# Attention and a top-k expert layer on one core: values in shorter pieces, wider DVE transposes, guard sums on two engines, and a new written order

## The chip, the cores and the metric

The kernel runs on one core of a Trainium2 chip. The metric is device time in microseconds (us): the median of several runs, and beside it one execution that the hardware profiler recorded. TensorE is called PE here (its weight loads PEld), VectorE DVE, ScalarE ACT, GpSimd POOL, SyncE SP.

## The reference

Attention over 8 batches of 8 heads, 576 tokens and 64 dimensions in float32, with rotary positions; then, in every batch, the 128 tokens with the highest gate score go through a two-layer network and are added back.

```python
q_rot, k_rot = rotate(q), rotate(k)
scores = scale * np.matmul(q_rot, k_rot.transpose(0, 1, 3, 2))
scores = scores - np.max(scores, axis=-1, keepdims=True)
attn = np.exp(scores)
attn = attn / (np.sum(attn, axis=-1, keepdims=True) + 1e-09)
x = np.matmul(attn, v)                       # per head, then heads side by side: (8, 576, 512)
...
scores[b] = x[b] @ w_gate
top_idx = np.argpartition(-scores[b], capacity)[:capacity]       # capacity = 128
h = np.maximum(x[b, top_idx] @ w1, 0.0)      # 512 -> 1024
out[b, top_idx] = x[b, top_idx] + sigmoid(scores[b, top_idx])[:, None] * (h @ w2)
```

## The kernel before

**Groups and units.** The 64 heads are worked in 16 groups of four (two groups make a batch), and a group is two pairs of heads, c = 0 and 1. A group has nine *units* u of 64 query columns for each pair. For a unit, `units` issues the score matmuls of both pairs (16 instructions on PE in tiles of 64x64, names `k_in` and `q_in`). For each of the two pairs `softmax` then drains the scores from PSUM, takes the row minimum of the negated scores (`nm`) and lets ACT make the exponentials with their sums (`prob`, `sums`). The table `DRAINS` says how a pair's unit is drained: "V" is one DVE instruction that drains and takes the minimum at once; "S" is a drain on ACT and a DVE reduction after it.

**Transposes.** The exponentials are transposed in place by DVE in 32x32 blocks, one instruction for both pairs of a unit (128x1152 elements); in the first units of groups 0 and 1 (`APART`) one for each pair.

**Values.** When all units of a group are transposed, `value` multiplies with the values: 18 key blocks, accumulated in four banks of PSUM, in tiles of 32x64 (names `prob`, `vt`), given to the order as three operations of six key blocks (96 matmul instructions each). ACT or DVE copies the sum out (`ot`), PE transposes it back with an identity (names `ident,ot`, whole array), and ACT or DVE scales the rows into `x`, by the reciprocals of the sums plus 1e-9: the *guard sums* (`guarded`, four small ACT additions, name `rs`) and a DVE reciprocal.

**Experts.** Behind every second group `route` and `chosen` pick the tokens (PE: `sc`, `past`, `tok`), POOL gathers their rows, and PE runs the two layers (names `xt,w1t` and `w2t,ht`, whole array). POOL also rotates k and q (`rotate`: a product with the table `tabk`, then an addition), and multiplies rows with the gate.

**What sets the order.** Nothing is scheduled at run time. All steps are recorded as operations, and the table `LINES` gives for each engine the order in which its operations stand, written as numbers in base 64. Every engine's queue is in order, and waits on semaphores for what the others make. `Order.run` replays that order with assumed durations; what it decides is which of the eight PSUM banks an operation gets. Its constants (`FETCH`, `SWITCH`, a restart price) are no part of the program that runs.

Almost all instructions carry the line of the helper that records them (L238 before, L243 after), so the rows below are told apart by tiles and shapes.

Of the kernel before, what the change touches and what calls it, by code (L numbers as in the profile page):

```python
# [13 lines left out]
ALU = mybir.AluOpType  # L14
# [11 lines left out]
BLOCK, FETCH = 256, 3600.0  # L26
# [13 lines left out]
6Z7B7t767364637I688O8R8W8Z95926c944L8Y978-6h8Q9c8T6j9e9b9i9k7H7G6l9n4K9x9p9A9E9r9v9C7U9K9I7W4PaJaG7YaB9RawaOaRau4Sb0aAb2  # L40
aIaLaTaDaQb8baaZbgbdaX9Q9PblbicFcCbpcScXcHbfbnb4cUcNd28rcRcEbw9WcZc-d6a1cLd9d4dca3dedjdbdidlbvbudwbBeh8qdreqdpdvdyelep8v
ejeBewbKeydFeDeFeseLeRePdDdEeUeJgodKgneYeWf1dR8ygtdTgqf3f0dVgvf7f9gxfggBgJcfgGgDgLgWgOgRg+gIgTh3gYh2h5gQhah9hcfeffhhhgi2
hjflici9i4ieibikiiiphqi6irfwioixivhphoiHiJhtiBiDkehCk7iNk9hEcmkliPhGkdkgiVknksiTkrkzkuf-kyj0kkkFkHkMkBkLkOkUkSi-i+kZkYk-
j5f+malNm1lYm9jcm5m3l6mclLlTmhlRl+mglXmnl4l5mjmtmpjglbmvg3mAldmCnSmznQlinYg6o2odmJo8o6lknWo0lmjLojocoqofopolovosoxozoDoF
mImHprpojKmMoMpxpqmZptpFpDoKoLpIpRpKoRpzpQpZpWpMjPq4pToPq6q3p-oYrzpYrxqcqarFqfo+qhqjrKqqrRnsp0rJrMrDrQrTrWr+rYs2s4qoqps7
sbs9qxnrsfskqCsnt2qEsht1t4nwtmqGt8tdsmtotattspnztBtytltItftvtAtDswtHthtstQtKtTtVtOsvtXsuu2szsBsIu0u1r9r8rduyrguxuC""",
    "DVE": """
0r0s0v0w0t0u0x0z0y0A0C0R0I0+0T1f17100K1o1h191q1x1A1H1F1b1C131j1O1J0W150N1l1M1t0Y331d2V1Q3a0P1v2G38351X3i2+2L2Q2I3f3p2X3n
3c3k2S3u3x3r303E3z3C5C3M3J595F3O5f5d573G5w5y5J5L2N5j5s5q5S5h5m5Z5Q5N5H5b5A5X5U5o6T6R3V6J6M6+5u6V797b5-7o7m726O7i7s7u667g
6Y7y7A4v7q757k4C4y4B4A4z7w704E7d6a7C8P774H8X937J968S8+4M989a909d8U9h9j9f9l9u9w9q7P9o9D7L7N9H9B9Jat9Fav9L9saH8baz9S9yaC8h  # L50
8g8f8i8eb3aSb1aWaYaKaxb9aPb7aMaEaUbha+bbbobm9U8kcGcQcDbecKcMcYcTc+8nbjb5d3bqd59YcI4Xd0cVcOd7dddabxdhdka5dfdmdodudqbz8sek
eibDdxeoevexbIdsdzeEemeCerezeIeKbMeGeteQb-eOdGeSeXeVgmc2dIc5c6gpdMc3eMe-c4eZf2gwf6f8c8gugrf4gAgygCcbfhfagKcg8DgZgEgPgHgS
gXgMh1h4g-h6h8hbgUhdhfhii5fjcefnhki3idiaihijfsiffuiqinili7hriwiuisiyiIfLiGhxiAiCiKhviOiMcjiEkck6k8kffOfSfPfRfQkjkmfUiUka
khiSkqktiWiQkxfXkEkGkvj1kAcrkIkKkNkokCkTkRg0kPkVkXk+lKlMj7j3l0m8m4lWlQm2lSmblZm6mfmdjemilOmmmolUl7l-msmumkmqnRl9nPmwmyjv
mBnXnVjyjzjAn-o1jBjCmDobnTo7o5jEjFo9oeoiokmKjHnZgbooo3orogjMoyowomotoAoCoEoGmOmQmVpwmXpyoNpspppEncpCpupGpLpJpPninfoTngnj
pSnhpAp+pNpXq5q2pUnlryrwq7qbjSq0q9rErAqdnoqiqgrCrIqkjXrPrSqrrLrNrGrZrUrXs1s3r-s5sas8sesgqvqtsct0slsot3t9t7sit5nttktgqVte
# [59 lines left out]
class Order:  # L116
# [36 lines left out]
    def run(self):  # L153
# [19 lines left out]
        while events:  # L173
# [4 lines left out]
            while moved:  # L178
                moved = False
                for e, line in lines.items():  # L180
                    while free[e] <= t and place[e] < len(line) and not line[place[e]].waits and able(e, line[place[e]]) <= t:
# [8 lines left out]
                        if e == "PE":  # L190
                            begin += SWITCH[mode][o.mode] + 70.0 * (t > free[e] + 1)
# [27 lines left out]
                        for n in o.outs:  # L219
                            n.ready = max(n.ready, o.end + self.SEM)  # L220
# [91 lines left out]
def attention_moe_kernel(ctx: ExitStack, tc: tile.TileContext, q, k, v, w_gate, w1, w2, rope, outs, cap):  # L312
# [67 lines left out]
    def pe(ns):  # L380
        return {"PE": (ns, ns + 165)}
# [77 lines left out]
    for t_ in rss.tiles:  # L459
# [5 lines left out]
    APART = {0: 6, 1: 3}  # L465
    DRAINS = (
        ("VVVVVSVSS", "SSSVVSSVV"),
        ("VSSSSSSSS", "SSSVSVSVS"),
        ("SVVVVVVSS", "VVSVVSVVV"),
        ("VSSVVSVVV", "SVVSVVVVV"),  # L470
        ("SSSVVSVSV", "SSSSVVVVV"),
        ("VVSSVSVSS", "VSSSVVVSV"),
        ("SVVSSSVVV", "SVSVVSSVS"),
        ("SVVSVVSVV", "VSVVVVVSV"),
        ("VSVSSSVVV", "SVVSSVSSS"),
        ("SSVVVVVVV", "VSVSVVVVV"),
        ("VVVVVVVVV", "VSSSSVSVS"),
        ("VVVSVVVVV", "VVSVSSVVS"),
        ("VVVVVVVSV", "VVVVSVSVV"),
        ("SVVSVSVVS", "SVVVSSSVV"),  # L480
        ("VVVVSVSVS", "VVSSVVVVS"),
        ("VVSVVSVVS", "SVVSSSSVV"),
# [38 lines left out]
    def rotate(pi):  # L521
# [12 lines left out]
        for name, use, tab, cuts in (("k", kin, tabk, CUTS), ("q", qin, tabk, QCUTS)):  # L534
            x = use.tile
# [519 lines left out]
```

## Time and profile before

| what | before |
|---|---|
| median of 3 runs | 514.68 us (513.63 to 515.67) |
| the profiled execution: its own time, its span | 514.91 us, 513.2 us |
| PE busy | 484.9 us, 94% |
| DVE busy | 449.5 us, 88% |
| ACT busy | 389.8 us, 76% |
| POOL busy | 340.8 us, 66% |
| granted PE clock, mean | 0.993 |

The profiled execution's own time is 1.7 us longer than the span from its first to its last instruction. Busy shares are means over the whole span; the windows further down give them by stage.

### The profile page before, as it was taken

How to read it: one execution, taken by the hardware profiler on the slowest of the kernel's cores; microseconds unless marked ns; L12 is line 12 of the kernel's file. 1: busy time of each engine (PE TensorE's matmuls, PEld its weight loads, DVE VectorE, ACT ScalarE, POOL GpSimd, SP SyncE). 2: the span in 40 equal slices, each digit the busy share in tenths (PEclk: the TensorE clock that was granted, in tenths of full speed). 3: DMA queues.
4: the chain of work that ended last, by engine and by line, in shares of the span. 5: the costliest groups of instructions: out<-in, count | busy, mean ns of one | idle time of the engine just before them, and what ended most of it. 6: DMA issues, size and time to landing. Idle time of an engine off the chain costs nothing.

```text
span 513.2 us, 19024 instructions
## 1 busy us (share of the span) xinstructions
PE 484.9 (94%) x7988; PEld 301.1 (59%) x7988; DVE 449.5 (88%) x871; ACT 389.8 (76%) x1087; POOL 340.8 (66%) x268
## 2 busy tenths in 40 slices
PE   8879787989999999998999999999999999999995
PEld 7446354555675556654558455674557456656872
DVE  6999999999999999999999999999779989991701
ACT  1799999999978989697887769887658778884110
POOL 2998398798793978758686795938587596006110
PEclk9989999899999999999999999999999999999999
DMA  8867676566445556363554536245563253130310
GB/s 288 286 185 221 186 232 204 157 195 190 139 121 150 152 167 196 89 209 105 167 160 142 170 101 216 67 127 164 176 190 118 75 178 84 58 101 23 114 42 20
DMA packets 47381, 76.52 MB, mean 149 GB/s; under 512 B 4928, under 2 KB 28224, under 8 KB 47296
## 3 DMA queue, kind: packets, MB, share of 16 engines
q1 hardware_dynamic: 45472, 70.54, 45.0%
q0 software_dynamic: 1280, 4.20, 2.4%
q8 instruction: 62, 1.02, 0.8%
q10 hardware_dynamic: 544, 0.59, 0.4%
q14 instruction: 23, 0.19, 0.1%
HBM read 63.77 MB, written 11.53 MB: 147 GB/s over the span
## 4 chain that ended last, share of the span: by engine, by line
PE 64%; ACT 12%; POOL 8%; issue 7%; DVE 6%; DMA 2%; SPq 1%; POOLq 0%; DVEq 0%
PE banks L238 64%; ACT prob L238 7%; DVE prob L238 5%; POOL k_in L238 4%; POOL q_in L238 3%; ACT ot L238 2%; ACT x L238 2%; DMA k_in<-k_dram 2%; SPq L238 1%; POOL prod L238 1%; ACT rs L238 0%; DVE nm L238 0%; ACT prod L238 0%; POOLq L1050 0%; POOL xe L238 0%
## 5 line engine op out<-in xcount | busy, mean ns | idle before, releaser
L238 ACT ACTIVATE prob<-prob,nm 128x576 f32<-128x576 f32 x288 | 220.7, 771 | 39.9 <-DVE prob L238 29.4
L238 DVE STREAM_TRANSPOSE prob<-prob 128x1152 f32<-128x1152 f32 (+1 forms) x153 | 194.1, 1288 | 4.4 <-ACT prob L238 4.0
L238 PE MATMUL banks<-k_in,q_in 64*64 64x288 f32 x2304 | 180.9, 419 | 17.3 <-DVE prob L238 7.0
L238 PE MATMUL banks<-prob,vt 32*64 32x288 f32 x4608 | 151.0, 405 | 2.1 <-ACT prob L238 2.0
L238 PEld LDWEIGHTS banks<-k_in,q_in 64*64 64x64 f32 x2304 | 83.5, 134 | 101.3 <-issue 25.4
L238 DVE TENSOR_SCALAR_CACHE_REDUCE prob<-banks 128x576 f32<-128x576 f32 x174 | 125.8, 742 | 11.9 <-PE banks L238 11.2
L238 PEld LDWEIGHTS banks<-prob,vt 32*64 32x64 f32 x4608 | 98.6, 132 | 51.1 <-issue 11.7
L238 POOL TENSOR_TENSOR q_in<-q_in,tabk 128x1152 f32<-128x1152 f32 (+1 forms) x32 | 82.8, 2592 | 15.3 <-DMA q_in<-q_dram 15.2
L238 POOL TENSOR_TENSOR k_in<-k_in,tabk 128x1152 f32<-128x1152 f32 (+1 forms) x31 | 81.1, 2618 | 12.6 <-DMA k_in<-k_dram 12.1
L238 ACT ACTIVATE prob<-banks 128x576 f32<-128x576 f32 x114 | 71.5, 647 | 22.9 <-PE banks L238 22.5
L238 POOL TENSOR_TENSOR prod<-x,wg 128x512 f32<-128x512 f32 (+1 forms) x45 | 49.3, 1096 | 56.0 <-ACT prod L238 17.4
L238 DVE TENSOR_REDUCE nm<-prob 128x1 f32<-128x576 f32 x114 | 81.5, 732 | 0.2
L238 PEld LDWEIGHTS banks<-xt,w1t 128*128 128x128 f32 x512 | 59.3, 192 | 8.0 <-issue 4.9
L238 PE MATMUL banks<-xt,w1t 128*128 128x128 f32 x512 | 63.1, 278 | 0.0
L238 PE MATMUL banks<-w2t,ht 128*128 128x512 f32 x128 | 61.6, 609 | 0.3 <-ACT ht L238 0.3
L238 ACT ACTIVATION_READ_ACCUMULATOR prob<-prob,nm 128x1 f32 x288 | 55.9, 194 | 0.0
L238 POOL TENSOR_TENSOR k_in<-k_in 128x576 f32<-128x576 f32 x31 | 43.8, 1414 | 0.9
L238 POOL TENSOR_TENSOR q_in<-q_in 128x576 f32<-128x576 f32 x31 | 43.8, 1417 | 0.9
L238 POOL TENSOR_SCALAR sel<-slots,rank 128x128 bf16<-128x128 bf16 x30 | 17.6, 599 | 38.8 <-DVE rank L238 38.8
L238 ACT ACTIVATE x<-banks,rs 128x64 f32<-128x64 f32 (+1 forms) x156 | 33.5, 333 | 4.5 <-PE banks L238 2.5
L238 PEld LDWEIGHTS banks<-w2t,ht 128*128 128x128 f32 x128 | 22.0, 189 | 23.3 <-issue 21.6
L238 ACT COPY ot<-banks 128x576 f32<-128x576 f32 x32 | 18.9, 638 | 10.8 <-PE banks L238 10.5
(68 smaller groups left out, 272.4 us busy)
## 6 DMA issues: line engine op xcount, KB each, us to landing
k_in<-k_dram SPq DMA_DIRECT2D x64, 288.0 KB, 3.6
vt<-v_dram SPq DMA_DIRECT2D x96, 192.0 KB, 2.9
q_in<-q_dram SPq DMA_DIRECT2D x62, 288.0 KB, 3.6
out_dram<-x SPq DMA_DIRECT2D x32, 256.0 KB, 3.5
w1t<-w_dram SPq DMA_DIRECT2D x8, 256.0 KB, 3.5
w2t<-w_dram SPq DMA_DIRECT2D x8, 256.0 KB, 3.4
out_dram<-x SPq DMA_DIRECT2D x16, 64.0 KB, 2.2
tabk<-rope_dram ACTq DMA_DIRECT2D x2, 288.0 KB, 3.6
```

Source lines behind the costliest of these rows:

```text
L238: i = made(*args, **kwargs)
```

## The change

Four things. The values of a group are recorded as six operations of three key blocks each (`STEP = 3`) and not three of six. In groups 1 to 14 DVE transposes two units at a time (`SPAN`, new helper `turn`), 128x2304 elements. The guard sums may stand on POOL as well as on ACT; the new table puts those of 8 of the 16 groups on POOL. And `LINES` and `DRAINS` are new: "S" drains go from 114 to 146 and "V" drains from 174 to 142. In the replay, an operation of a sum that stands behind another of PE may now start as soon as PE is free.

```diff
+RESTART = (70.0, 130.0, 70.0)
...
+    SPAN = {g: 2 for g in range(1, 15)}
+    STEP = 3
...
-            part = prob.tile[:, cs[0] * NU + u:cs[-1] * NU + u + 1:NU]
-            y = op({"DVE": dve(len(cs) * S, 1, 26.0)}, lambda: nc.vector.transpose(part, part),
-                   [exps[c, u] for c in cs])
+        def turn(cs, u0, u1):
+            part = prob.tile.rearrange("p (c u) s -> p c u s", c=2)[:, cs[0]:cs[-1] + 1, u0:u1]
+            part = part[:, 0] if len(cs) == 1 else part[:, :, 0] if u1 - u0 == 1 else part
+            y = op({"DVE": dve(len(cs) * (u1 - u0) * S, 1, 26.0)}, lambda: nc.vector.transpose(part, part),
+                   [exps[c, u] for c in cs for u in range(u0, u1)])
             prob.by(y)
             turned.append(y)
...
-            for i in range(3):
-                o = op(pe(CH * 485), lambda i=i: products(i), turned + vt[i][1] + [o], acc, mode=1,
-                       words=32 * CH)
+            for k0 in range(0, NB, STEP):
+                use, got = vt[k0 // CH]
+                o = op(pe(STEP * 485), stream(k0, k0 + STEP), turned + got + [o], acc, mode=1, words=32 * STEP)
+                prob.by(o), use.by(o)
...
-                        nc.scalar.add(r[64 * half:64 * half + 64, 0:n, 2 * h:2 * h + 2].rearrange("p t c -> p c t"),
-                                      su[64 * h:64 * h + 64, :, half:NU:2], EPS)
-
-            gd = op({"ACT": (800, 905)}, guarded, list(exps.values()) + rs.before)
+                        to = r[64 * half:64 * half + 64, 0:n, 2 * h:2 * h + 2].rearrange("p t c -> p c t")
+                        of = su[64 * h:64 * h + 64, :, half:NU:2]
+                        if e == "ACT":
+                            nc.scalar.add(to, of, EPS)
+                        else:
+                            nc.gpsimd.tensor_scalar(to, of, EPS, None, op0=ALU.add)
+
+            gd = op({"ACT": (800, 905), "POOL": (560, 560)}, guarded, list(exps.values()) + rs.before)
...
         for u in range(NU):
-            for cs in ((0,), (1,)) if u < APART.get(g, 0) else ((0, 1),):
+            apart = u < APART.get(g, 0)
+            for cs in ((0,), (1,)) if apart else ((0, 1),):
                 units(cs, u)
+                if apart:
+                    turn(cs, u, u + 1)
+        lo = APART.get(g, 0)
+        while lo < NU:
+            hi = min(lo + SPAN.get(g, 1), NU)
+            turn((0, 1), lo, hi)
+            lo = hi
```

What the new order does is seen best in three places.

On PE, where the first layer of batch 4 begins (`sc` is batch 5's routing scores, `ot` the rows to be transposed back, `w1t` the first layer), there stood before one half of a token block's products, a unit of scores, and the next half:

```order
L238 MATMUL banks<-ident,sc_104 128x128 x5
L238 MATMUL banks<-ident,ot_88 128x128 x4
L238 MATMUL banks<-xt_100,w1t 128x128 x8
L238 MATMUL banks<-k_in_80,q_in_76 64x288
...
L238 MATMUL banks<-k_in_81,q_in_77 64x288
L238 MATMUL banks<-xt_100,w1t 128x128 x8
```

Now 24 of the first layer's matmuls stand together:

```order
L243 MATMUL banks<-ident,sc_104 128x128 x5
L243 MATMUL banks<-ident,ot_88 128x128 x4
L243 MATMUL banks<-ident,ot_88 64x128 x2
L243 MATMUL banks<-xt_100,w1t 128x128 x24
L243 MATMUL banks<-ident,ot_88 128x128 x4
L243 MATMUL banks<-k_in_78,q_in_74 64x288
```

The scores that stood between the pieces have gone ahead of them, into one run. Counted over all of PE's order, the changes from one tile size to another (128x128, 64x64, 32x64) go from 186 to 167: 17 fewer between scores and whole-array work, 2 fewer at values. Of the 19, 4 are gone in groups 0 to 7 and 15 in groups 8 to 15.

On DVE, in the middle of group 6 (`prob_86` is the buffer of the even groups), the transposes of two units now stand as one instruction between the drains:

```order
L243 STREAM_TRANSPOSE prob_86<-prob_86 128x2x1152
L243 TENSOR_SCALAR prob_86,nm_93<-banks 128x576 x2
L243 STREAM_TRANSPOSE prob_86<-prob_86 128x2x1152
L243 TENSOR_SCALAR prob_86,nm_93<-banks 128x576 x2
L243 STREAM_TRANSPOSE prob_86<-prob_86 128x2x1152
```

Before, no instruction of 128x2x1152 was there. Over the kernel 110 transposes of 128x2x576 become 55 of 128x2x1152; 25 of 128x2x576 and 18 of 128x576 remain.

On POOL, among the rotations of k and q for groups 1 and 2, the order before was:

```order
L238 TENSOR_TENSOR k_in_80<-k_in_80 128x576
L238 TENSOR_TENSOR k_in_78<-k_in_78,tabk 128x1152
L238 TENSOR_TENSOR k_in_78<-k_in_78 128x576
L238 TENSOR_TENSOR q_in_74<-q_in_74,tabk 128x1152
L238 TENSOR_TENSOR q_in_75<-q_in_75,tabk 128x1152
```

Now the guard sums of group 0 stand between them:

```order
L243 TENSOR_TENSOR k_in_80<-k_in_80 128x576
L243 TENSOR_TENSOR k_in_78<-k_in_78,tabk 128x1152
L243 TENSOR_SCALAR rs_95<-sums_91 64x2x5 x2
L243 TENSOR_SCALAR rs_95<-sums_91 64x2x4 x2
L243 TENSOR_TENSOR q_in_74<-q_in_74,tabk 128x1152
```

The four additions have moved from ACT's queue into POOL's, behind a rotation. Further up in POOL's queue the addition for `q_in_75` of group 0 is gone; it stands on DVE now.

## Rows read from the trace of the kernel before

**Rows 1.** Busy time by stage: window, its length, PE, PEld, DVE, ACT, POOL.

```profile
12.00:34.00 22.00, 17.06 (x150) 8.20 (x146) 22.00 (x41) 18.30 (x43) 21.84 (x13) 1.00 0.76 251
34.00:130.00 96.00, 85.39 (x1745) 50.16 (x1749) 94.13 (x166) 92.33 (x271) 77.68 (x52) 0.96 0.66 196
130.00:230.00 100.00, 98.83 (x1619) 61.94 (x1612) 95.94 (x178) 86.91 (x242) 74.20 (x60) 1.00 0.51 152
230.00:460.00 230.00, 225.40 (x3903) 138.25 (x3901) 213.87 (x409) 181.39 (x502) 151.03 (x111) 1.00 0.44 135
460.00:513.20 53.20, 47.63 (x519) 33.11 (x518) 15.86 (x56) 9.60 (x34) 13.31 (x23) 1.00 0.14 48
```

**Rows 2.** Waits, whole span: who waited for whom, us, times, longest.

```profile
DVE prob L238 <- PE banks L238: 11.2, 27, 0.9
...
PE banks L238 <- DVE prob L238: 7.0, 11, 1.8
```

**Rows 3.** Timeline of PE, value stretches: start, length, what, count.

```profile
41.14 3.17 PE L238 MATMUL banks<-prob,vt 32*64 32x288 f32 x96
44.23 1.20 PE L238 MATMUL banks<-k_in,q_in 64*64 64x288 f32 x16
...
71.73 8.99 PE L238 MATMUL banks<-prob,vt 32*64 32x288 f32 x288
80.64 1.20 PE L238 MATMUL banks<-k_in,q_in 64*64 64x288 f32 x16
```

**Rows 4.** Timeline of PE, an expert stretch.

```profile
270.71 1.95 PE L238 MATMUL banks<-xt,w1t 128*128 128x128 f32 x16
272.49 0.60 PE L238 MATMUL banks<-ident,ot 128*128 128x128 f32 x4
273.02 1.20 PE L238 MATMUL banks<-k_in,q_in 64*64 64x288 f32 x16
274.15 2.05 PE L238 MATMUL banks<-xt,w1t 128*128 128x128 f32 x16
276.14 2.17 PE L238 MATMUL banks<-k_in,q_in 64*64 64x288 f32 x32
278.24 2.05 PE L238 MATMUL banks<-xt,w1t 128*128 128x128 f32 x16
```

**Rows 5.** Timeline of DVE around 28 us.

```profile
27.48 1.36 DVE L238 STREAM_TRANSPOSE prob<-prob 128x1152 f32<-128x1152 f32 x1
...
28.77 0.70 DVE L238 TENSOR_REDUCE nm<-prob 128x1 f32<-128x576 f32 x1
...
29.41 0.76 DVE L238 STREAM_TRANSPOSE prob<-prob 128x576 f32<-128x576 f32 x1
...
30.09 0.70 DVE L238 TENSOR_REDUCE nm<-prob 128x1 f32<-128x576 f32 x1
```

**Rows 6.** Timeline of ACT around 38 us; the bracket is idle time before.

```profile
36.41 0.91 ACT L238 ACTIVATE rs<-sums 64x10 f32<-64x10 f32 x4
38.23 1.19 ACT L238 ACTIVATE prob<-banks 128x576 f32<-128x576 f32 x2 [0.90 <-PE banks L238]
```

**Rows 7.** Groups by shape, DVE and ACT: busy us, mean ns, idle before.

```profile
L238 DVE TENSOR_SCALAR_CACHE_REDUCE prob<-banks 128x576 f32<-128x576 f32 x174 | 125.8, 742 | 11.9 <-PE banks L238 11.2 <-ACT prob L238 0.2
L238 DVE TENSOR_REDUCE nm<-prob 128x1 f32<-128x576 f32 x114 | 81.5, 732 | 0.2
...
L238 ACT ACTIVATE prob<-banks 128x576 f32<-128x576 f32 x114 | 71.5, 647 | 22.9 <-PE banks L238 22.5
```

**Rows 8.** Groups by shape, POOL.

```profile
L238 POOL TENSOR_TENSOR k_in<-k_in,tabk 128x1152 f32<-128x1152 f32 x30 | 79.7, 2657 | 4.3 <-DMA k_in<-k_dram 3.9 <-issue 0.3
...
L238 POOL TENSOR_TENSOR q_in<-q_in 128x576 f32<-128x576 f32 x31 | 43.8, 1417 | 0.9
L238 POOL TENSOR_SCALAR sel<-slots,rank 128x128 bf16<-128x128 bf16 x30 | 17.6, 599 | 38.8 <-DVE rank L238 38.8
...
L238 POOL CAST tok<-sc 128x5 bf16<-128x5 f32 x8 | 1.6, 203 | 0.0
```

More of the change, by code (lines that the diff above doesn't have):

```diff
@@ L40 @@
[L40 to L44, printed above, removed]
@@ new lines @@
+iCiFhAiTiIiRhEhCj1kqiZiMkikkf+iXg1f-g0g2j2g4kDkBkokukIkxkGl5j3g7jdkOkMkRcDl7kXkUk+l6l8l1l3lZjhjfjjmfl9ljm6mjgcm3mdlXm9mm
+jqm1mpmsmMmxmvmLmNmDjHmAllo2mOmGobmJohjOo9o5jKlpjMjLjNonoQozjQotolmPorofoEoCoxgnjToRoJoHjYoSmZoMoOoToUpIm-lwpGn3lyn8pOna
+pSpVpMncnrq8qbp-q2p2pZq5nuqwnwnvnyqenxqxrPnArSqhqyqoqlnDrVrXqzqsnIqur+qAk7sDs8s1s5sdsbsEsjsgqKsFspsnssqOqMqQsvsBszqVtntq
+tlsGuatttGrctEtxrhrgsHrfrjritAtQsRtKtWtZtNubu3uetTu1ucu6u8ufudrluhuiugsVsTt0usroupuquuuwuyuAuCrtt4uzuBuDuHnTuKuMuNuOuLuQ
+uRuTuYuWrEv7""",
@@ L219, in run @@
                         for n in o.outs:
-                            n.ready = max(n.ready, o.end + self.SEM)
+                            n.ready = max(n.ready, free[e] if e == "PE" and "PE" in n.engines else o.end + self.SEM)
                             n.waits -= 1
@@ L465, in attention_moe_kernel @@
     APART = {0: 6, 1: 3}
+    SPAN = {g: 2 for g in range(1, 15)}
+    STEP = 3
     DRAINS = (
[L467 to L482, printed above, removed]
+        ("VVVVVSSSS", "SVSSSVSVS"),
+        ("SSVSSSSSV", "SVSSSSVSS"),
+        ("VVSVSVVVS", "SSSSSVSVV"),
+        ("VVSSVSSVV", "VVSSVSSSV"),
+        ("SSSVVVVSV", "SSSVSVSVV"),
+        ("SSSSVSSVV", "VSSSSVSVS"),
+        ("SSVSVVVSV", "SVVSVVVVS"),
+        ("VSVSVVSSV", "SSSVSVSVV"),
+        ("VVSSSSSVS", "SVVSVVVVV"),
+        ("SSSVVVSVS", "VVSVSSVVV"),
+        ("VSSSVSVVV", "VVSVVVSSV"),
+        ("SSVSSVVVV", "VVSVSSVSS"),
+        ("VSSSSSVVV", "SVVVVVVVV"),
+        ("SSSSVVVSS", "VVSVSSSSV"),
+        ("VVVSVVSVS", "SVSSVSVSV"),
+        ("SVSSSVVSV", "VSSVSSSVV"),
     )
@@ L534, in rotate @@
         for name, use, tab, cuts in (("k", kin, tabk, CUTS), ("q", qin, tabk, QCUTS)):
+            ready = tab_ready
             x = use.tile
@@ L540, in rotate @@
                     y = [tt(hi - lo, x[:, w, lo:hi], x[:, w, lo:hi], tab[:, w, lo:hi], ALU.mult,
-                            [got[name][w]] + tab_ready, use, both) for w in range(2)]
+                            [got[name][w]] + ready, use, both) for w in range(2)]
                 else:
@@ L544, in rotate @@
                             [got[name][i]] + [t for t, c, d in zip(tab_ready, CUTS, CUTS[1:]) if lo < d and c < hi] if first
-                            else got[name] + tab_ready, use, both)]
+                            else got[name] + ready, use, both)]
                 made[name].append((lo, hi, tt(
@@ L568, in units @@
                     for c in cs:
-                        half = r ^ c
-                        kin, qin, _ = pairs[c]
-                        mms.append((c, slice(64 * half, 64 * half + 64), n,
-                                    qin.tile[rows, 0, u * 64:u * 64 + 64], kin.tile[rows, 0, n * HALF:n * HALF + HALF]))
+                        kin, qin = pairs[c][0].tile, pairs[c][1].tile
+                        mms.append((c, r ^ c, n, qin[rows, 0, u * 64:u * 64 + 64], kin[rows, 0, n * HALF:n * HALF + HALF], True, True))
             def products():
-                for c, to, n, lt, rt in mms:
-                    nc.tensor.matmul(bank_of(bs[c])[to, n, 0:HALF], lt, rt, start=True, stop=True)
-            room = prob.before + nm.before + sums.before
+                for c, half, n, lt, rt, first, last in mms:
+                    nc.tensor.matmul(bank_of(bs[c])[64 * half:64 * half + 64, n, 0:HALF], lt, rt, start=first, stop=last)
+            room = prob.before + nm.before + sums.before + ([] if g else [warming])
             needs = [o for c in cs for name in "kq" for lo, hi, o in pairs[c][2][name]
@@ L610, in softmax @@
             else:
-                d = op({"ACT": act(S)}, drained, [o] + prob.before, b)
+                d = op({"ACT": act(S, 10)}, drained, [o] + prob.before, b)
                 m = op({"DVE": dve(S)}, lowest, [d] + nm.before)
@@ L625, in value, with streamed @@
             ot, rs = ots.next(), rss.next()
-            def products(i):
-                for kb in range(i * CH, i * CH + CH):
+            def streamed(k0, k1):
+                for kb in range(k0, k1):
                     for a in range(4):
```

73 lines of the change are left out of this document (38 added, 35 removed).

## The prediction

> **What bounds the kernel now.** I read the busy time by stage first, since the shares of the whole span hide that three engines take turns [rows 1]. From 12 to 230 us DVE is busy 22.00 + 94.13 + 95.94 = 212.1 of 218 us, 97%, and from 34 to 130 us ACT is at 92.33 of 96 as well, while PE stands at 85.39 of 96. The softmax sets the pace there, and PE waits for it. From 130 us on PE takes over, because the experts join: 98.83 of 100, then 225.40 of 230, then the end, which is expert work on PE with the other engines nearly idle. DVE stays close behind (213.87 of 230 between 230 and 460 us). So a saving on PE counts from about 130 us on, and a saving on DVE or ACT counts before that; one that helps neither place shows nowhere. The waits say the same from both sides: DVE waited 11.2 us in 27 pieces for scores, and PE 7.0 us in 11 pieces for DVE's drains [rows 2].
>
> Second I read what PE's busy time is made of, because "busy" there includes the changes of tile size. Starts of neighbouring rows are the measure, since a row's own length overlaps with the next. 288 value matmuls take 80.64 - 71.73 = 8.91 us, and 96 followed by scores take 44.23 - 41.14 = 3.09 [rows 3]. The difference is 5.82 us for 192 matmuls, 30.3 ns each, so 96 alone are 2.91 and the step from values to scores costs 0.18 us. A unit of scores between two expert pieces takes 274.15 - 273.02 = 1.13, two in a row 278.24 - 276.14 = 2.10 [rows 4]; so a unit is 0.97 and the step out of scores costs 0.16. Sixteen matmuls of the first layer take 272.49 - 270.71 = 1.78 where whole-array work follows and 276.14 - 274.15 = 1.99 where scores follow: 0.21 for the step into scores. Behind the transposes with the identity that step costs less: four take 273.02 - 272.49 = 0.53, and the same work at the first layer's 111 ns each (1.78 / 16) would be 0.45, so about 0.08.
>
> **The change, part by part.**
>
> *Tile changes on PE.* The order has 17 fewer changes between scores and whole-array work: 8 out of scores and 9 into them. The 8 cost 0.16 each, 1.3 us. Of the 9, five stood behind layer products (0.21) or routing work, four behind identity transposes (0.08); between 9 x 0.08 and 9 x 0.21, 0.7 to 1.9, I take 1.2. The two fewer at values are 0.3. Sum: 2.8 us less on PE, bounds 2.3 to 3.5. Since 15 of the 19 are in groups 8 to 15, where PE is at 98%, nearly all of it should reach the end.
>
> *Shorter value pieces.* They add no instruction. Where scores come between pieces they cost the two steps above, and the count already has them. What 288 matmuls in one run show is that PE does not stop between parts of one sum [rows 3], so longer runs, such as 72 source matmuls, cost nothing either.
>
> *Transposes of two units.* A transpose of 1152 elements keeps DVE 28.77 - 27.48 = 1.29 us, one of 576 elements 30.09 - 29.41 = 0.68 [rows 5]. Twice the size costs 0.61 more, so 0.07 us of each is fixed, and one of 2304 should take 2.51 (estimate from these two). 55 of the 110 fixed parts go: 55 x 0.07 = 3.9 us of DVE time. Bounds: nothing if the larger shape has a cost of its own, 3.9 otherwise; I take 3.9. The Trainium skill, "Perfetto Trace Analysis", section "Optimizing Scalar/DVE Operations", gives about 60 ns of such overhead for DVE on SBUF and advises grouping where the engine is saturated; by its figure the saving would be 3.3 us (estimate), and no term of the sum changes.
>
> *32 more drains on ACT.* The DVE instruction is 742 ns before and 732 after [rows 7], so DVE gets 0.3 us back in all. ACT pays a drain of its own; the second of two in a row costs 1.19 - 0.65 = 0.54 us, with 1.19 for two and 0.65 from the mean of one [rows 6, 7]: 32 x 0.54 = 17 us over the kernel. Half of the guard sums, 8 x 0.91 = 7.3 us [rows 6], and 40 of 156 small row scalings go the other way. ACT has 230 - 181.4 = 49 us of idle after 230 us, so what is left of the 9.7 is hidden there. But the load is not even: until the last exponential of group 3 the new order has 12 more drains (6.5 us) and three fewer guard sums (2.7) in ACT's queue: 3.8 us more, where it has 96 - 92.33 = 3.7 us of idle [rows 1]. This is cover that just suffices; without it the cost is up to 3.8 us.
>
> *Guard sums on POOL.* The trace has no such instruction on POOL. The nearest are a cast of 128x5 at 203 ns and a comparison of 128x128 at 599 [rows 8]; at 20 elements a row the first is nearer, so four take 0.8 us, bounds 0.8 to 2.4. They can stand behind a rotation of 2.66 us. Behind them wait the rest of POOL's queue and a DVE reciprocal; in the new order DVE has other work ahead of that reciprocal, and POOL is busy only 151.03 of 230 us. I take nothing; were each late by a rotation, 8 x 2.66 = 21 us of DVE time would be the far bound.
>
> *The start.* One addition of 1.42 us leaves POOL's queue [rows 8], ahead of the k for group 1, for which PE and, behind it, the drains wait. It lands on DVE, which is full from 12 to 34 us [rows 1]. ACT stood idle 0.90 us behind that wait [rows 6]; DVE pays some 0.64, as for a reduction of 576 elements (29.41 - 28.77) [rows 5]. Net nothing, 0.9 us either way.
>
> *DVE before 230 us.* I added up DVE's queue in both orders by these prices up to group 7's last transpose: the new one is 0.4 us shorter, because transposes of wider shape are few in the first two groups and work from elsewhere has moved ahead. So of DVE's 3.9 only 0.4 counts; the rest falls where DVE has 230 - 213.9 = 16 us of idle.
>
> **Sum.** 514.9 - 2.8 - 0.4 = 511.7 us against the profiled execution, which is 0.2 above the median. I say 511.6. A measurement of this kernel can tell about 0.5%, 2.6 us, from no change, and this is a change of 3.1.
>
> **Rivals.**
>
> *A larger gain.* Pieces of 24 or 72 source matmuls let the order put a unit of scores where DVE needs it; before, DVE had 96 instructions, 3.1 us, to sit through at most. DVE's 11.2 us of waiting for scores [rows 2] is what could be had. A third of it, 3.7 us, gives 508; all of it, with the rest, 500. Against: the units of scores before each group's values are nearly the same in number in both orders.
>
> *No gain.* ACT's 3.8 us in the first 130 us run into an engine that has 3.7 left [rows 1]; with waits that can't be closed up, the softmax of groups 2 and 3 comes 2 to 4 us later, PE has no spare work yet, and the saving is given back: 514.5. Against: DVE, with 94.13 of 96, is as full as ACT there, and a transpose that stands in DVE's queue anyway doesn't care whether its exponentials come a little later.
>
> *Slower: the long transpose.* A drain that is queued behind a transpose now waits up to 2.51 us and not 1.29, and with it a PSUM bank that PE wants. The same section of the skill warns that where DVE isn't saturated but makes others wait, breaking instructions up lets work finish sooner; this change does the reverse. Here PE's waits for DVE are 7.0 us in 11 pieces [rows 2]. 55 long transposes that each pass 0.06 us on to PE cancel the gain; from 0.11 us each, 5.9 us, the kernel is slower by over 0.5%. One in ten passing its whole 1.22 us on is 6.7 us: 518. For it: no slack on DVE before 230 us. Against: DVE runs 97% full at 1.29 us pieces and passes little on, and more drains are on ACT now.
>
> **How the numbers follow.** The forecast, 509.8 to 513.4, gets 0.40; the larger gain, below 509.8, 0.20; no gain, 513.4 to 517, 0.28; slower by the long transpose, 0.12. From 507 to 517 leaves out a good third of the larger gain (0.08) and most of the slower case (0.10). Faster by over 0.5% means below 512.1: the 0.20 and two thirds of the 0.40, so 0.47; slower by over 0.5%, above 517.3, is 0.12; the rest, 0.41, is the same.
>
> **What would show it.** Right: PE's order ran with 167 tile changes and the prices above, so PE's busy time is about 2.8 us less with the same work; transposes of 2304 elements at a pitch near 2.5 us; value runs of 144 instructions at 30 ns each; POOL's guard sums near 0.2 us each and no long wait of a reciprocal behind them. Wrong: more PE waits for DVE than 7 us (the long transpose); ACT without idle from 34 to 130 us while DVE has more than 2 us of it (ACT); DVE's waits for scores well under 11 us (the larger gain); or value runs that stop inside, which would mean that instructions don't come fast enough.

## The result and the profile after

The changed kernel takes 518.20 us (median of 18 runs, 515.74 to 522.05) against 514.79 us of the kernel before in the same comparison: a ratio of 1.007 (95% interval 1.0053 to 1.0086). It is slower by 3.4 us where 3.1 us less was forecast, and it lies above the forecast's range. Its profiled execution took 518.34 us, with a span of 516.6 us and a mean granted clock of 0.987.

The windows by stage of the changed kernel (window, its length, PE, PEld, DVE, ACT, POOL, granted clock, DMA share, GB/s) answer to [rows 1]:

```profile
12.00:34.00 22.00, 17.60 (x143) 10.48 (x143) 20.07 (x34) 15.03 (x34) 21.00 (x12) 0.84 0.79 247
34.00:130.00 96.00, 81.67 (x1709) 48.14 (x1709) 93.76 (x142) 92.03 (x254) 75.33 (x60) 0.98 0.62 185
130.00:230.00 100.00, 98.55 (x1636) 62.10 (x1629) 94.73 (x163) 90.44 (x249) 74.31 (x59) 1.00 0.50 149
230.00:460.00 230.00, 225.59 (x3869) 138.65 (x3875) 210.99 (x357) 184.43 (x480) 163.71 (x144) 1.00 0.46 140
```

The first line is the one to look at. Before, DVE had no idle time between 12 and 34 us; now 1.93 us of it are idle, ACT does 3.3 us less, and the granted clock is 0.84. The value matmuls of group 0 begin at 44.84 us and not at 41.14 [rows 3], 3.7 us late, and that is about the size of the whole loss.

Three timelines of the changed kernel show how it comes about: start, length, instruction, and in brackets the idle time before it. On DVE:

```profile
16.05 0.75 DVE L243 TENSOR_REDUCE nm<-prob 128x1 f32<-128x576 f32 x1
16.79 3.16 DVE L243 TENSOR_TENSOR q_in<-q_in 128x576 f32<-128x576 f32 x1
19.88 2.08 DVE L243 STREAM_TRANSPOSE prob<-prob 128x576 f32<-128x576 f32 x3
```

On POOL:

```profile
13.99 2.77 POOL L243 TENSOR_TENSOR q_in<-q_in,tabk 128x576 f32<-128x576 f32 x2
16.72 2.62 POOL L243 TENSOR_TENSOR k_in<-k_in,tabk 128x1152 f32<-128x1152 f32 x1
19.42 1.80 POOL L243 TENSOR_TENSOR k_in<-k_in 128x576 f32<-128x576 f32 x1
```

On PE:

```profile
11.83 3.78 PE L243 MATMUL banks<-k_in,q_in 64*64 64x288 f32 x27
20.01 6.39 PE L243 MATMUL banks<-k_in,q_in 64*64 64x288 f32 x44 [4.40 <-DVE q_in L243]
...
37.46 1.20 PE L243 MATMUL banks<-k_in,q_in 64*64 64x288 f32 x16 [2.87 <-POOL k_in L243]
...
44.84 1.71 PE L243 MATMUL banks<-prob,vt 32*64 32x288 f32 x48
```

The moved addition stands on DVE for 3.16 us. POOL's second q product ends at about 16.7, which makes the addition ready; POOL goes straight on with its 128x1152 product for group 1, and DVE's addition ends 0.6 us after that product does (16.72 + 2.62 = 19.34, against 19.95). POOL's next addition is longer too, 1.80 us where the same one takes 1.42 in a kernel below without the overlap. PE has nothing else to do and waits 4.40 us.

PE's clock then falls. Windows of two microseconds of the changed kernel, with the granted clock as the first number behind POOL's:

```profile
18.00:20.00 2.00, 0.00 (x0) 0.00 (x0) 2.00 (x2) 0.46 (x2) 1.92 (x2) 0.68 0.70 207
20.00:22.00 2.00, 1.99 (x19) 1.06 (x23) 1.96 (x3) 0.00 (x0) 2.00 (x2) 0.50 0.68 196
22.00:24.00 2.00, 2.00 (x20) 1.05 (x14) 0.75 (x1) 1.75 (x4) 2.00 (x2) 0.50 0.84 239
24.00:26.00 2.00, 2.00 (x17) 1.12 (x14) 1.55 (x4) 2.00 (x6) 2.00 (x1) 0.61 0.81 216
26.00:28.00 2.00, 2.00 (x28) 1.29 (x24) 2.00 (x5) 1.10 (x4) 2.00 (x3) 1.00 0.65 238
```

By the windows at 0.68 and 0.61 the granted clock is at half, 1.2 of 2.4 GHz, from about 18.7 to 25.6 us: it falls while PE waits, and PE's first 5.6 us of work behind the wait run at it. DVE now waits for scores in a stretch in which it had no idle time to give. The kernel before has no such fall there, its clock is 1.00 from 12 to 34 us [rows 1]; its wait for the same scores was 0.62 us.

What PE itself does came out as forecast, by an estimate. I cut PE's time from its first to its last matmul, start to start, into work at unit prices (60.6 ns a score matmul, 30.3 a value matmul, 112 one of the first layer, and so on, the same for both kernels), the price of each kind of tile change, and the rest, which is waiting. Work is 419.9 us in both. Tile changes, counted in each order at these prices, go from 30.7 to 27.9 us. Waiting, which is what is left, goes from 48.9 to 55.0 us: 3.7 of the 6.1 more lie ahead of group 0's values, 1.3 fewer between 41 and 97 us, 3.6 more between 97 and 460 us. The sum is, but for rounding, the 3.4 us between the two spans. PE's busy time does not show the saving, 484.8 us against 484.9, for it also holds matmuls at half clock; in the profile of the first kernel below, at a clock of 1.00 from 5 to 460 us, it is 480.1.

### The profile page after: what moved, and what is told of

Its sections match the earlier page's. It is cut to its first block, busy times and chain, and to the rows that moved or that the text cites. A ratio compares the mean times of both kernels' runs of the same rounds, so it can differ in the third digit from the quotient of the medians.

```text
span 516.6 us, 18965 instructions
## 1 busy us (share of the span) xinstructions
PE 484.8 (94%) x7988; PEld 303.3 (59%) x7988; DVE 449.5 (87%) x781; ACT 392.0 (76%) x1040; POOL 349.9 (68%) x304
## 4 chain that ended last, share of the span: by engine, by line
PE 42%; POOL 10%; issue 9%; ACT 6%; DVE 4%; DMA 3%; POOLq 0%; ACTq 0%; DVEq 0%; SPq 0%
PE banks L243 42%; POOL k_in L243 3%; POOL q_in L243 3%; ACT prob L243 3%; POOL prod L243 2%; DVE prob L243 2%; ACT ot L243 2%; DVE nm L243 1%; DMA q_in<-q_dram 1%; DMA k_in<-k_dram 1%; ACT prod L243 1%; DVE past L243 0%; POOL xe L243 0%; POOL out_dram L243 0%; ACT ht L243 0%
## 5 line engine op out<-in xcount | busy, mean ns | idle before, releaser
L243 DVE STREAM_TRANSPOSE prob<-prob 128x2304 f32<-128x2304 f32 (+2 forms) x98 | 187.1, 1926 | 3.7 <-ACT prob L243 3.5
L243 PEld LDWEIGHTS banks<-k_in,q_in 64*64 64x64 f32 x2304 | 86.8, 134 | 106.7 <-ACT prob L243 23.0
L243 DVE TENSOR_SCALAR_CACHE_REDUCE prob<-banks 128x576 f32<-128x576 f32 x142 | 103.9, 746 | 13.5 <-PE banks L243 10.5
L243 ACT ACTIVATE prob<-banks 128x576 f32<-128x576 f32 x146 | 92.2, 653 | 28.9 <-PE banks L243 28.4
L243 DVE TENSOR_REDUCE nm<-prob 128x1 f32<-128x576 f32 x146 | 103.6, 738 | 3.4 <-ACT prob L243 3.1
L243 POOL TENSOR_TENSOR q_in<-q_in,tabk 128x1152 f32<-128x1152 f32 (+1 forms) x32 | 82.3, 2578 | 14.8 <-DMA q_in<-q_dram 14.5
L243 PE MATMUL banks<-xt,w1t 128*128 128x128 f32 x512 | 61.5, 277 | 0.1
L243 POOL TENSOR_SCALAR sel<-slots,rank 128x128 bf16<-128x128 bf16 x35 | 20.6, 608 | 40.0 <-DVE rank L243 40.0
L243 POOL TENSOR_TENSOR q_in<-q_in 128x576 f32<-128x576 f32 x30 | 42.6, 1425 | 0.4
L243 ACT ACTIVATE prod<-prod 128x256 f32<-128x256 f32 (+1 forms) x54 | 22.0, 411 | 8.5 <-POOL prod L243 8.4
L243 POOL DMA_INDIRECT out_dram<-xe,idx x8 | 8.3, 1040 | 29.6 <-DVE xe L243 28.8
```

Of the source, the lines that this page charges most:

```text
L243: i = made(*args, **kwargs)
```

## The experiments

The change and the first four kernels behind it ran beside a kernel before of 514.8 us, the others on two other chips, where it took 517.5 and 517.6 us. So ratios are what can be compared. The profiles place most of these 2.7 us in the value matmuls: start to start within their runs they add up to 133.3 us in the kernel before, and to 136.3 in the same kernel with one filler on such a chip (134.3 in the changed kernel, 137.6 where POOL waits for the addition). Why, no run shows.

| kernel | median us | ratio to before | 95% interval |
|---|---|---|---|
| the change | 518.20 | 1.0070 | 1.0053 to 1.0086 |
| addition on POOL | 516.09 | 1.0016 | 0.9990 to 1.0042 |
| before, addition on DVE | 517.48 | 1.0037 | 1.0016 to 1.0058 |
| guard sums on ACT | 521.09 | 1.0113 | 1.0093 to 1.0133 |
| short transposes | 518.65 | 1.0074 | 1.0054 to 1.0093 |
| the change, two fillers | 523.31 | 1.0113 | 1.0083 to 1.0143 |
| addition on POOL, two fillers | 519.47 | 1.0034 | 1.0011 to 1.0057 |
| before, one filler | 520.34 | 1.0056 | 1.0039 to 1.0073 |
| POOL waits for the addition | 516.68 | 0.9984 | 0.9965 to 1.0002 |
| the change, one filler | 519.54 | 1.0031 | 1.0017 to 1.0045 |
| POOL waits, guard sums of group 13 on ACT | 515.67 | 0.9954 | 0.9935 to 0.9974 |
| the same, with two short fillers | 514.21 | 0.9930 | 0.9914 to 0.9946 |

My theory (A) was the collision of the moved addition with POOL's product. The rivals were POOL's queue standing behind the guard sums (B) and the long transposes (C).

**The addition back on POOL.** `0G` is q_in_75's addition, `0F` its last product, `2G` the k product of group 1.

```diff
 "POOL"
-0B0D0E0F2G2H...
+0B0D0E0F0G2G2H...
 "DVE"
-...0Z1p0G1h1r...
+...0Z1p1h1r...
```

> The changed kernel, with one thing undone: the q addition of pair 1 (q_in_75, one instruction of 128x576) stands on GpSimd again, right behind its two products, ahead of the k product for group 1. Theory A (the moved addition collides with GpSimd's 128x1152 product: it took 3.16 us on DVE where about 0.65 was costed, PE waited 4.40 us for it, and group 0's values began 3.7 us later than before): PE's wait for that addition shrinks to some 2.5 us, group 0's values begin near 42 us instead of 44.84, and the time falls by 2.5 to 3.7 us, to 514.5 to 515.7. Theory B (guard sums on GpSimd hold its queue up) and theory C (transposes of two units hold drains up) expect 518 as it is, since neither is touched; by them the start only fills a wait that comes again later.

Timeline of PE in this kernel's profiled execution:

```profile
18.24 4.11 PE L243 MATMUL banks<-k_in,q_in 64*64 64x288 f32 x46 [2.69 <-POOL q_in L243]
...
34.40 5.10 PE L243 MATMUL banks<-k_in,q_in 64*64 64x288 f32 x56 [2.33 <-POOL k_in L243]
39.42 1.71 PE L243 MATMUL banks<-prob,vt 32*64 32x288 f32 x48
```

That execution took 513.15 us, with group 0's values 5.4 us earlier than in the changed kernel. But the 12 runs lie apart: four at 511.97 to 513.15 us, with a mean clock of 0.995 to 0.998, and eight at 515.93 to 518.68 us with 0.984 to 0.991. The median is 2.1 us better than the change, less than the 2.5 to 3.7 that were expected. So A holds for the place, and a second thing takes part that goes along with the clock.

**The kernel before, with the addition on DVE.**

```diff
 "POOL"
-0B0F0E0D0G2B...
+0B0D0E0F2B...
 "DVE"
-...0K1o1h19...
+...0K1o0G1h19...
```

> The kernel before, with this one part of the change alone: GpSimd's order for pair 1 is that of the changed kernel (k product, k addition, q products) and the q addition of pair 1 stands on DVE behind the row minimum of unit 5, as in the changed kernel. Theory A: the addition lasts about 3 us on DVE instead of 0.65, since GpSimd begins its 128x1152 product at the moment the addition becomes ready; group 0's values begin 2.5 to 3.7 us later than 41.14, and the time is 517 to 518.5. Theories B and C: within 1 us of the kernel before, since GpSimd is relieved of 1.4 us as DVE pays 0.65.

DVE's addition in this kernel:

```profile
18.39 2.04 DVE L238 TENSOR_TENSOR q_in<-q_in 128x576 f32<-128x576 f32 x1
```

and what POOL did beside it:

```profile
17.19 2.63 POOL L238 TENSOR_TENSOR k_in<-k_in,tabk 128x1152 f32<-128x1152 f32 x1 [0.47 <-DMA k_in<-k_dram]
19.77 3.16 POOL L238 TENSOR_TENSOR q_in<-q_in,tabk 128x1152 f32<-128x1152 f32 x1
```

Here the addition comes 1.2 us after POOL's product, and it is shorter by as much: again it ends 0.6 us after the product (19.82 and 20.43). PE waits 3.26 us for it and not 0.62. The one part alone, the addition together with the changed kernel's order of POOL for pair 1, costs 0.37% and moves group 0's values from 41.14 to 43.55 us. It is shown, then, that this part of the change makes the kernel before slower.

**All guard sums on ACT.** `1-`, `3Z`, `6d`, `fs`, `hz`, `li`, `qJ`, `sQ` move from POOL's line to ACT's, a few places behind the last exponential of their group:

```diff
 "POOL"
-...2D521-5453...
+...2D525453...
```

> The changed kernel with all sixteen groups' guard sums on ACT (eight of them moved back from GpSimd, each a few instructions behind the last exponential of its group); everything else, the addition on DVE too, stays. Theory B (GpSimd's queue stands behind guard sums that wait for the last exponential, 17.0 us in 4 waits, so rotations of k come late and PE waits for them): waits of PE for k get shorter and the time falls by 2 to 3 us, to 515 to 516. Theory A: GpSimd has the time, the start is as it was; ACT gets 7 us more work in all, 2.7 of it before 100 us where it is nearly full, so 517.5 to 519.5. Theory C: 518.

2.9 us slower than the change. B falls as a whole: taking all these waits from POOL makes the time longer. It is longer than theory A expected too, 521.09 against 517.5 to 519.5; in this profile the clock is 0.91 from 34 to 130 us, where the change has 0.98, and what of the loss is ACT's load and what the clock stays open.

**Short transposes.**

```diff
-    SPAN = {g: 2 for g in range(1, 15)}
+    SPAN = {}
```

with each of the 55 numbers replaced by two that follow each other in DVE's line.

> The changed kernel with every transpose of two units (128x2304) split into two of one unit (128x1152) at the same place of DVE's queue, 55 more instructions; everything else stays. Theory C (drains and the first score banks wait behind the long transposes): less waiting, 514.5 to 516.5. Theories A and B: the 55 fixed parts of 0.07 to 0.08 us come back on DVE, of which some tenths reach the end before 230 us and most are hidden after it: 518 to 519.5.

No difference to the change that can be told (1.0074 and 1.0070). C falls, and the long transposes bring nothing that can be measured either.

**Fillers in PE's waits.** What goes along with the clock divides A: the delay alone (A1), or the delay and the half clock behind it (A2). To keep PE at work without making anything ready earlier, I put identity matmuls ahead of a unit's own, into the bank that the unit overwrites.

```diff
             def products():
+                for _ in range({(0, 6, (0, 1)): 24, (1, 4, (0, 1)): 16}.get((g, u, cs), 0)):
+                    nc.tensor.matmul(bank_of(bs[cs[0]])[:, 0, 0:P], ident, ident, start=True, stop=True)
```

> The changed kernel, the addition still on DVE, with matmuls of the identity put where PE waits in the start: 24 ahead of the first unit that needs pair 1 (it waited 4.40 us) and 16 ahead of the unit of group 1 that waits 2.87 us; they write the bank that the unit then overwrites. Nothing that the softmax needs becomes ready earlier by it. Theory A1 (the collision delays everything by its own 2.5 us and the delay alone makes the loss): 518 as it is, or later where a filler runs past the wait. Theory A2 (the long wait also lets PE's clock fall to half speed, 6.83 us of it in the changed kernel's trace, and scores at half speed make the rest of the loss): the stretch from 18 to 26 us stays at full clock, the clock over the run is 0.995 or more, and the time falls by 1.5 to 3 us, to 515.2 to 516.7.

> The kernel with the q addition of pair 1 back on GpSimd (its runs lay at 512.0 to 513.2 us where the mean clock was 0.995 or more, and at 515.9 to 518.7 where it was 0.984 to 0.991), with 14 identity matmuls ahead of the first unit that needs pair 1 (it waited 2.69 us) and 12 ahead of the unit of group 1 that waited 2.33 us. Theory A2 (the clock falls behind such a wait in some executions and costs 3 to 4 us then): all runs at a clock of 0.994 or more and between 511.5 and 513.5 us, faster than the kernel before. Theory A1 (the clock only goes along with some other lateness): the spread from 512 to 518 stays, median 516.

> The kernel before with 14 identity matmuls ahead of the unit of group 1 for which PE waited 2.82 us at 34.45 us. A control for the two kernels above: the kernel before waits only 0.62 us for pair 1, so theory A2 gives a gain of at most what its own falls of the clock cost, 0.5 to 1 us (513.7 to 514.3; its runs at a clock of 0.998 lay at 513.4 to 514.8). Theory A1: 514.75, no change. A gain of over 2 us would say that the fillers do something else.

All three came out slower than the same kernel without them, by 0.4, 0.2 and 0.6%; for the second the intervals overlap widely, for the first a little. PE's timeline of the first of them tells why:

```profile
14.73 5.62 PE L243 MATMUL banks<-ident 128*128 128x128 f32 x48
20.29 3.89 PE L243 MATMUL banks<-k_in,q_in 64*64 64x288 f32 x46
...
35.10 5.44 PE L243 MATMUL banks<-ident 128*128 128x128 f32 x32 [2.92 <-DVE prob L243]
```

A filler takes 0.23 us (5.62 / 24, two rows each). And the second place is no free wait: the fillers there need no k, and still waited 2.92 us, for the drain of the bank they write to, and then took 5.44 us. So the wait of 2.87 us at 37.46 in the changed kernel, which the view puts down to POOL's k, is one for a drain: there the last k of group 1 was ready at 33.24 us, and a drain ended at 37.30:

```profile
31.82 1.42 POOL L243 TENSOR_TENSOR k_in<-k_in 128x576 f32<-128x576 f32 x1
...
36.56 0.74 DVE L243 TENSOR_SCALAR_CACHE_REDUCE prob<-banks 128x576 f32<-128x576 f32 x1
```

These runs are inconclusive on the clock, but the first place kept it at 1.00 from 12 to 34 us.

**POOL waits for the addition.** `held` is the addition; the k product of group 1 is given a semaphore wait for it.

```diff
+        if id(o) in held_:
+            tc.add_manual_dep(mine[0], made[id(held_[id(o)])][-1].name, ...)
...
-                            else got[name] + ready, use, both)]
+                            else got[name] + ready + held, use, both)]
```

> The changed kernel, the addition on DVE as it is, but GpSimd's first product for group 1 (128x1152) waits for it with a semaphore, so that no GpSimd instruction runs beside it. Theory A (DVE's addition stands still until GpSimd's running product ends: in the changed kernel the product ended at 19.34 and the addition at 19.95, in the kernel before with the addition on DVE at 19.82 and 20.43): the addition lasts 0.45 to 0.75 us instead of 3.16, PE's wait for it is about 2 us instead of 4.40, GpSimd begins some 0.7 us later but runs undisturbed, and the time is 512 to 516, as with the addition on GpSimd or better. If the addition is slow for its own sake (both inputs in SBUF, whatever GpSimd does), it still lasts 2 to 3 us and the time is 518 or more, since GpSimd now waits too.

DVE's timeline of this kernel:

```profile
16.55 0.75 DVE L243 TENSOR_TENSOR q_in<-q_in 128x576 f32<-128x576 f32 x1
17.22 2.09 DVE L243 STREAM_TRANSPOSE prob<-prob 128x576 f32<-128x576 f32 x3
```

and POOL's:

```profile
17.38 2.65 POOL L243 TENSOR_TENSOR k_in<-k_in,tabk 128x1152 f32<-128x1152 f32 x1 [0.99 <-DVE q_in L243]
```

The same addition at the same place takes 0.75 us, 0.67 to the next start, which is what the prediction had costed. POOL pays 0.99 us. From 1.0070 to 0.9984 is 4.4 us, with intervals that don't meet: the collision, with all that follows it, accounts for the whole loss of 3.6 us (0.70%) and 0.8 us more. Its profile shows PE's wait at 17.36 down to 1.72 us.

**One filler, sized to the wait.** 15 and not 24, and none at the second place.

> The changed kernel, the addition on DVE beside GpSimd's product as it is, with 15 identity matmuls (0.23 us each in the kernels filled before, 3.5 us) ahead of the first unit that needs pair 1 and none elsewhere. In the kernel with two fillers this place kept full clock from 14 to 34 us, but the second filler itself took 5.44 us behind PE's wait and hid what the first was worth. Theory A2 (the fall of the clock behind the 4.40 us wait costs some 1.2 us between the first unit of pair 1 and the first unit of both pairs of group 1, 17.45 us in the changed kernel against 16.2 at full clock): that stretch takes 16.0 to 16.5 us, and the time is 1 to 2.5 us under the changed kernel's, a ratio of 1.002 to 1.005 to the kernel before. Theory A1 (only the addition's own delay counts): the ratio stays at 1.007.

PE's timeline of this kernel:

```profile
14.88 3.62 PE L243 MATMUL banks<-ident 128*128 128x128 f32 x30
18.43 0.70 PE L243 MATMUL banks<-k_in,q_in 64*64 64x288 f32 x2
19.83 11.87 PE L243 MATMUL banks<-k_in,q_in 64*64 64x288 f32 x118 [0.70 <-DVE q_in L243]
34.62 1.20 PE L243 MATMUL banks<-k_in,q_in 64*64 64x288 f32 x16 [2.92 <-DVE prob L243]
```

The addition still holds pair 1 back until 19.83, but from there to the first unit of both pairs of group 1 it is 14.8 us and not 17.45, less than I had expected, and the time falls by 0.39%, 2.0 us, with intervals that don't meet. The addition became ready hardly earlier (19.83 against 20.01); only PE was kept at work. So about 2 of the 4.4 us are the clock that falls behind the wait (1 to 3 by the two intervals), and by subtraction the other 2.4 the delay itself.

**The guard sums of group 13 on ACT.** POOL of the changed kernel at this place, in its timeline:

```profile
411.14 1.11 POOL L243 DMA_INDIRECT xe<-out_dram,idx  x1 [0.28 <-POOL idx L243]
412.55 0.27 POOL L243 TENSOR_SCALAR rs<-sums 64x10 f32<-64x10 f32 x1 [0.30 <-ACT prob L243]
415.64 0.86 POOL L243 TENSOR_SCALAR rs<-sums 64x10 f32<-64x10 f32 x3 [2.82 <-DMA xe<-out_dram,idx]
416.58 5.29 POOL L243 TENSOR_TENSOR q_in<-q_in,tabk 128x1152 f32<-128x1152 f32 x2
```

The second of the four stands 2.82 us behind the gather that POOL itself had just issued: it reads nothing of the gathered rows, but in the trace it waits for the semaphore that their transfer raises when it lands, at 415.56 us. The last group's rotations stand behind it. PE waits for them 18 us later:

```profile
430.43 1.20 PE L243 MATMUL banks<-k_in,q_in 64*64 64x288 f32 x16
433.57 2.17 PE L243 MATMUL banks<-k_in,q_in 64*64 64x288 f32 x32 [1.94 <-POOL k_in L243]
```

The edit, on top of the kernel in which POOL waits:

```diff
 "POOL"
-penEqJthtd...
+penEthtd...
 "ACT"
-...qvpfs0s7...
+...qvpfqJs0s7...
```

> The kernel in which GpSimd waits for the addition on DVE, and in which besides the guard sums of group 13 alone stand on ACT again, behind the last exponential of that group. In that kernel's trace the first of these four instructions ran at 410.62 us on GpSimd and the second at 413.56, after 2.67 us of waiting for the gather of rows that GpSimd had issued just ahead of it; the rotations of the last group stood behind them, and PE waited 1.77 us for k at 431.45. Theory D (this guard sum is what takes part of the saving on PE back): the wait at 431 us is gone or under 0.5 us, and the time falls by 1 to 2 us, to a ratio of 0.994 to 0.997. Rival: the wait for k has another cause (its load, or GpSimd's load as a whole), or the time is lost again in the last two groups: no change, 0.998.

PE at the same place now, with all 48 score matmuls in one run and no wait among them:

```profile
428.85 3.43 PE L243 MATMUL banks<-k_in,q_in 64*64 64x288 f32 x48
432.23 3.84 PE L243 MATMUL banks<-xt,w1t 128*128 128x128 f32 x32
```

The ratio goes from 0.9984 to 0.9954, 1.5 us. The two intervals overlap a little, so it is the row and not the time alone on which this rests. This kernel is faster than the kernel before, by 0.3 to 0.7% by its interval.

**The same with two short fillers.**

```diff
+                for _ in range({(0, 6, (0, 1)): 5, (1, 2, (1,)): 4}.get((g, u, cs), 0)):
```

> The kernel with the guard sums of group 13 on ACT and GpSimd waiting for the addition, with 5 identity matmuls (1.2 us) ahead of the first unit that needs pair 1, where PE waits 1.72 us, and 4 (0.9 us) ahead of the unit of group 1 where it waits 1.82 us. Theory A2: fewer executions in which the clock falls in the first 45 us, a mean clock over 0.993 in most, and 0 to 2 us less than without them. Rival (the fillers stand behind a PSUM bank and not in the wait, as the second one of the earlier kernels did): 0.5 to 1.5 us more than without them.

Windows of this kernel, where the changed one has 0.57, 1.00 and 0.84 as its clock, and the kernel without the fillers 1.00, 1.00 and 0.84:

```profile
18.00:26.00 8.00, 8.00 (x86) 4.56 (x78) 8.00 (x16) 7.58 (x19) 7.92 (x4) 1.00 0.79 214
26.00:34.00 8.00, 4.91 (x42) 2.92 (x44) 8.00 (x12) 7.84 (x20) 7.57 (x6) 1.00 0.84 285
34.00:45.00 11.00, 11.00 (x215) 5.96 (x212) 10.55 (x17) 10.59 (x25) 9.84 (x8) 1.00 0.79 250
```

0.9930, 0.7% faster than the kernel before (0.5 to 0.9%), the best of all; five of its six runs have a mean clock of 0.995 or more. Against the kernel without the fillers it is 1.2 us, within what the intervals leave open.

## Why the prediction was wrong

**The step that failed is "The start".** It said of the moved addition: POOL saves 1.42, DVE pays some 0.64, "net nothing, 0.9 us either way". It priced the addition by a reduction of 576 elements, an instruction with one input, alone on its engine. The addition has two inputs in SBUF, and POOL's product that stands next in its queue reads SBUF as well; both become startable by the same event, POOL is there first, and DVE stands still for the product's whole length. That is a price of 2.5 us over the 0.64. The kernel in which POOL waits shows it directly: 0.75 against 3.16 us for the same instruction. With what follows it is 4.4 us, nearly five times the bound that I gave.

The Trainium skill, "SBUF — State Buffer", section "Who interferes with whom", states this rule: a DVE instruction with two SBUF inputs contends with a GpSimd instruction that reads SBUF, what they share is an exclusive lock, and the order of issue decides who blocks. The rows agree (the addition ended 0.6 us after POOL's product in both kernels, though it had started 0.07 us behind the product in one and 1.2 us in the other). It would have been the rule that speaks against this change, and the prediction did not weigh it.

The trace of before had it, too. There DVE's first k product of pair 1 (128x576, the same shape with two inputs) started just behind a POOL product, and took 1.96 us, to 0.6 us after the product's end:

```profile
10.94 1.96 DVE L238 TENSOR_TENSOR k_in<-k_in,tabk 128x576 f32<-128x576 f32 x1
...
10.83 1.45 POOL L238 TENSOR_TENSOR k_in<-k_in,tabk 128x576 f32<-128x576 f32 x1 [8.23 <-DMA k_in<-k_dram]
```

In the changed kernel, where it starts ahead of POOL's (10.39 and 10.56 us), it takes 0.75, and it is POOL's product that is longer, 1.85 us and not 1.45.

**The wait that the failed step makes costs twice.** The price of a clock fall can be read from one and the same stretch, 56 score matmuls from the first unit of both pairs of group 1 to group 0's values. At full clock it takes 5.02 us (addition on POOL, 34.40 to 39.42) and 5.03 (the best kernel), and with a fall behind the wait ahead of it 6.69 (the kernel in which POOL waits, 33.61 to 40.30): 1.67 us.

```profile
33.61 6.76 PE L243 MATMUL banks<-k_in,q_in 64*64 64x288 f32 x56 [2.34 <-POOL k_in L243]
40.30 1.71 PE L243 MATMUL banks<-prob,vt 32*64 32x288 f32 x48
```

The kernel before pays the same 1.67 us itself (34.45 to 41.14 [rows 3]); its clock is 0.84 from 34 to 45 us, and with the filler, at full clock, it takes 5.01 for this stretch (37.28 to 42.29):

```profile
34.45 6.76 PE L238 MATMUL banks<-k_in,q_in 64*64 64x288 f32 x56 [2.82 <-POOL k_in L238]
```

[rows 1] have the clock of 0.96 there, and the prediction makes nothing of it. In the changed kernel there are two such falls ahead of group 0's values and not one.

**Tile changes on PE: right, as far as an estimate goes.** There are 167 changes, and 2.8 us less by the sum above, as forecast; that is a count at the forecast's own prices, and no run measures it by itself. It did not all reach the end of this kernel: between 97 and 460 us PE waited 3.6 us more, of which 1.94 are the wait at 433.57 us.

**Shorter value pieces: right but for 0.9 us.** Most value runs hold at 30.3 ns per matmul. Two don't: 192 matmuls from 303.96 us take 6.55 us to the next scores where 6.00 would be due, and 144 from 366.11 us take 4.88 where 4.54 would. No single stop in them is as long as 0.15 us, and what slows them no run shows.

**Transposes of two units: right in size, and without effect.** Two of them take 252.60 - 247.64 = 4.96 us, 2.48 each, where 2.51 was forecast, on DVE's timeline of the changed kernel:

```profile
247.64 5.03 DVE L243 STREAM_TRANSPOSE prob<-prob 128x2304 f32<-128x2304 f32 x2
252.60 0.72 DVE L243 TENSOR_SCALAR_CACHE_REDUCE prob<-banks 128x576 f32<-128x576 f32 x1
```

With short ones DVE is busy 452.5 us and not 449.5, so 3.0 us were saved where 3.9 were forecast. Of these the prediction counted 0.4, and undoing them changes the time by 0.04%, below what can be told.

**Guard sums on POOL: wrong for one group of eight.** They take 0.3 us each and not 0.2. "I take nothing" fails for group 13, where a gather stands just ahead: about 1.5 us. The other seven no run takes one by one; all eight together are worth more on POOL than on ACT. The prediction's far bound had them late by a rotation each; what made one late was a transfer.

**32 more drains on ACT, and DVE before 230 us: not the cause.** Between 34 and 130 us ACT is as busy as before (92.03 and 92.33) and DVE's idle time is 2.24 us and not 1.87. The kernel in which POOL waits has the same drains and is not slower than the kernel before. The rival "no gain" looked for the loss at groups 2 and 3; it lies ahead of group 0's values.

**The long transpose: not the cause.** PE's waits for DVE's drains fell from 7.0 us to 1.9:

```profile
PE banks L243 <- POOL k_in L243: 5.0, 3, 2.9
...
PE banks L243 <- DVE q_in L243: 4.4, 1, 4.4
...
PE banks L243 <- DVE prob L243: 1.9, 3, 1.0
```

With the wait of 2.87 us that the view counts as one for k, those for drains are 4.8 us, still less than before. The new entry of 4.4 us in one piece is the failed step. No rival of the prediction had it.

With the two waits taken away the sum of the prediction nearly comes out: 0.9954 of 514.8 is 512.4 us, against 511.6 (by its own terms, 514.7 - 2.8 - 0.4, it is 511.5). What the remaining 0.8 us are is not settled. That is within the interval (0.9935 to 0.9974), and PE has other waits between 97 and 400 us, each under 1.4 us, that no run took apart. It bears the other terms out only as a sum: no run shows each of them at the end.

## What to carry to other kernels

When an instruction moves from one engine to another, its price is not that of its shape alone: look at what the engine it came from will start at the same moment, and whether the two can run side by side. A wait that PE has in a full pipeline can cost more than its length, since half clock may follow; the granted clock in the windows of before shows where it falls already, but not where a new wait will make it fall (it was 1.00 from 12 to 34 us). And filling a wait helps only where the filler's own needs are met: a filler that waits for a bank only adds its length.

## What the runs showed of the hardware

A DVE addition of 128x576 with two SBUF inputs takes 0.67 us from start to start by itself. Started 0.07 or 1.2 us behind a POOL product of 128x1152 that reads SBUF, it ended 0.6 us after that product. PE's clock fell to half behind waits of 4.40 us (the changed kernel), 2.82 (the kernel before) and 2.34 (the kernel in which POOL waits, where it fell once more behind one of 1.70 at 61.20 us); it stayed at 1.00 behind waits of 2.69 and 2.33 (addition on POOL) and 2.34 (the best kernel, with fillers in the two waits ahead of it). So the length of the one wait did not decide it. The addition-on-POOL kernel, whose profiled execution had these two waits and no fall up to 460 us, had a mean clock from 0.984 to 0.998 in 12 runs, and 6.7 us between them in time. I had not expected such a spread from one program.
